# Seven products instead of eight in the down projection of two more chunks, with weights cast in place and later loads

## Chip, cores and metric

One core of one Trainium2 chip (trn2). The metric is the device time of the whole kernel in microseconds (us). A time quoted as a median is the median of a kernel's runs; a span or a duration comes from one profiled execution.

## The reference, cut to what matters

```python
def reference(A_x, A_k_cache, A_v_cache, A_wq, A_wo, B_x, B_w_gate, B_w_up, B_w_down):
    # x: 2048 x 448; 16 query heads, 8 K/V heads of width 256; F = 1792
    xn = layernorm(x)
    # attention: softmax((xn @ wq) k^T / 16) v over the last 512 keys, then @ wo
    s = attention(xn, k_cache, v_cache, wq, wo)
    g = silu((gelu(xn @ w_gate) * (xn @ w_up)) @ w_down)
    return x + s * g
```

The change concerns `... @ w_down` (the "down" product, 1792 to 448), with its silu, called the gates below. The 2048 tokens are worked on in four chunks, 0 to 3, of 512.

## The kernel before

One program lists operations; a helper works out the waits from the buffers that each operation reads and writes. Every engine then carries out its own list in that order. The order in the text is therefore the order in each engine's queue. In the cuts `bank` is the memory into which TensorE writes its results; an eviction is an operation of VectorE or ScalarE that reads a finished bank, after which the bank can be used again.

The plan is: gate and up products of all four chunks, with the down products of chunks 0 and 1 in between; then attention, head by head, for each chunk. The down products of chunks 2 and 3 come in the first two heads of attention, to give TensorE work until the first softmaxes are done.

Chunks 0, 2 and 3 use the plain form, four tiles of 128 tokens with 14 matmuls of 448 columns each:

```python
def down(c, pairs):
    for t4 in range(4):
        ...
        mms([(bank[b][:, 0:D], actT[:, c % 2, f, t4 * P:(t4 + 1) * P], wd[:, f, :], f == 0, f == NF - 1)
             for f in range(NF)], [b_wd] + b_actT[c % 2], (b_ps[b],))
        act(tmp[:, s, 0:D], bank[b][:, 0:D], ACT.Tanh, ...)      # ScalarE
        K.op("dve", ...)                                         # VectorE: the gate
        dma("sp", g2d[t], g2w[t4], ...)
```

Chunk 1 already uses seven products of half size in place of eight (Strassen's scheme in Winograd's form). Some products take sums of activation blocks (`sd`) or of weight blocks (`wdt` 3 to 6), which VectorE makes ahead. `product` is 14 matmuls of 224 columns:

```python
def down7(c, one, other):
    ...
    product(0, B1, A(0, 0))
    act(U2, bank[B1][:, 0:D], ACT.Copy, (b_ps[B1],), bU2, scale=F)   # ScalarE copies product 0
    product(5, B6, S(2))
    product(6, B7, S(3))
    product(3, B4, A(1, 1))
    product(4, B5, S(0))
    product(2, B3, S(1))
    product(1, B1, A(1, 0), False)                                   # adds to product 0's bank
    ... # VectorE evictions, ScalarE tanh, gates
```

A head's scores: four tiles, each of which ScalarE exponentiates into one of three f32 buffers and VectorE then normalizes; the tile is transposed by a DMA on SP's queue. The products with V of a head come two heads later (`LAG = 2`).

```python
def s_mm(m):
    for t4 in range(4):
        b = AB[t4]
        mms([... qT, kT ...], ..., (b_ps[b],))
        n = m * 4 + t4
        r, z, y, x = n % NRS, n % NP32, n // 2 % NPN, n // 4 % NPT       # NP32 = 3
        # ScalarE: p32[:, z, :] = exp(bank[b])
        if t4 % 2 == 1:
            # VectorE: reciprocal of two sums; pn[:, y, t, :] = p32 * reciprocal, for both tiles
            dma_t(pT[...], pn[...], ...)                                # SP: transposed copy
...
for m in range(NS):
    if m in groups:                      # 0, 4, 12, 18, ...: a query stage for the next heads
        ... q_group(...)
    s_mm(m)
    if m < LAG:
        down(NQC - LAG + m, nxt)         # chunks 2 and 3
    ...
    if len(late) == LAG:
        pv(late.pop(0))
```

The softmax here doesn't subtract the row's maximum and nothing guards it: scores larger than these inputs give would overflow.

## Time and profile before

| | before |
|---|---|
| median (3 runs, 545.04 to 546.44) | 546.26 us |
| profiled span | 543.6 us |
| TensorE busy | 538.5 us, 99% |
| down stage of chunk 1 (seven products) | 9.50 us |
| down stages of chunks 2 and 3 (plain) | 10.59 us each |
| heads 2 and 3, up to the second query stage | 7.00 us |

First the busy times by engine and the chain of waits that ended last, from the page of the kernel before:

```profile
PE 538.5 (99%) x4022; PEld 298.2 (55%) x4022; DVE 361.6 (67%) x803; ACT 311.9 (57%) x780; POOL 39.2 (7%) x78
PE 95%; DMA 2%; DVE 1%; ACT 1%; issue 0%; DVEq 0%; ACTq 0%
```

TensorE bounds the kernel nearly everywhere. The windows view of the kernel before, over the stages that the change touches; columns: stretch, its length and PE's busy time in it, then PEld, DVE, ACT, POOL with counts, PE's clock, DMA share, GB/s:

```profile
78.81:88.31 9.50, 9.50 (x101) 9.32 (x100) 6.96 (x12) 3.52 (x7) 0.00 (x0) 1.00 0.01 3
120.37:130.96 10.59, 10.59 (x57) 5.48 (x56) 3.96 (x9) 3.06 (x9) 0.00 (x0) 1.00 0.51 119
132.69:143.28 10.59, 10.59 (x57) 5.48 (x56) 3.96 (x9) 3.12 (x9) 0.00 (x0) 1.00 0.34 92
143.28:150.28 7.00, 7.00 (x33) 3.04 (x32) 4.49 (x12) 6.10 (x19) 2.92 (x5) 1.00 0.46 106
```

Rows are chunk 1's stage, chunk 2's, chunk 3's, and heads 2 and 3. PE is busy throughout, at full clock. The seven-product stage is 1.09 us shorter than a plain one. Two places in the timeline of before: VectorE's last weight sum for chunk 1, and ScalarE around head 1's last two exponentials:

```profile
80.35 0.96 DVE L368 TENSOR_TENSOR wdt<-wdt 128x1568 f16<-128x1568 f16 x1
132.80 0.61 ACT L817 ACTIVATE p<-bank 128x512 f32<-128x512 f32 x1
133.67 0.60 ACT L817 ACTIVATE p<-bank 128x512 f32<-128x512 f32 x1 [0.17 <-DVE pn L824]
135.53 0.54 ACT L365 ACTIVATE tmp<-bank 128x448 f32<-128x448 f32 x1 [1.18 <-PE bank L374]
```

The weight sum ends at 81.31, 2.5 us after the stage began; product 3, which reads it, comes fourth and does not wait. The fourth exponential waits 0.17 us for a normalization (`pn`) that frees its f32 buffer.

### The profile page before, as it was taken

How to read it: one execution, taken by the hardware profiler on the slowest of the kernel's cores; microseconds unless marked ns; L12 is line 12 of the kernel's file. 1: busy time of each engine (PE TensorE's matmuls, PEld its weight loads, DVE VectorE, ACT ScalarE, POOL GpSimd, SP SyncE). 2: the span in 40 equal slices, each digit the busy share in tenths (PEclk: the TensorE clock that was granted, in tenths of full speed). 3: DMA queues.
4: the chain of work that ended last, by engine and by line, in shares of the span. 5: the costliest groups of instructions: out<-in, count | busy, mean ns of one | idle time of the engine just before them, and what ended most of it. 6: DMA issues, size and time to landing. Idle time of an engine off the chain costs nothing.

```text
span 543.6 us, 10604 instructions
## 1 busy us (share of the span) xinstructions
PE 538.5 (99%) x4022; PEld 298.2 (55%) x4022; DVE 361.6 (67%) x803; ACT 311.9 (57%) x780; POOL 39.2 (7%) x78
## 2 busy tenths in 40 slices
PE   8999999999999999999999999999999999999997
PEld 5554457445444444884444469544444984444487
DVE  6673886783457757844775786367667844776775
ACT  5433664873448858206875860488488116877820
POOL 1130400000100000003001000120000003001010
PEclk9999999999999999999999999999999999999999
DMA  9569272993345716402961760068447403773811
GB/s 297 122 189 126 56 128 88 291 237 87 88 93 116 156 44 150 79 1 69 164 156 42 144 151 1 18 145 147 97 105 154 62 1 78 161 150 83 153 49 35
DMA packets 171459, 61.36 MB, mean 113 GB/s; under 512 B 154960, under 2 KB 168272, under 8 KB 171408
## 3 DMA queue, kind: packets, MB, share of 16 engines
q1 hardware_dynamic: 167632, 51.39, 44.4%
q0 software_dynamic: 3008, 8.72, 6.9%
q8 instruction: 32, 0.52, 0.4%
q10 hardware_dynamic: 768, 0.57, 0.3%
q14 instruction: 19, 0.16, 0.1%
HBM read 19.76 MB, written 3.67 MB: 43 GB/s over the span
## 4 chain that ended last, share of the span: by engine, by line
PE 95%; DMA 2%; DVE 1%; ACT 1%; issue 0%; DVEq 0%; ACTq 0%
PE bank L374 95%; DMA pT<-pn 2%; ACT p L817 1%; DVE pn L824 1%; DMA x<-in_A_x_dram 0%; DVE stats L421 0%; ACT qT L365 0%; PE bank L472 0%; DVE rden L821 0%; DVE oTh L842 0%; ACT oTh L365 0%; DVE xn L447 0%; ACT xnT L365 0%; DVE mv L424 0%; PE bank L491 0%
## 5 line engine op out<-in xcount | busy, mean ns | idle before, releaser
L817 ACT ACTIVATE p<-bank 128x512 f32<-128x512 f32 x256 | 150.4, 596 | 25.2 <-DVE pn L824 22.4
L374 PE MATMUL bank<-kT,qT 128*128 128x512 bf16 x512 | 121.1, 379 | 0.0
L374 PE MATMUL bank<-pT,va 128*128 128x512 bf16 x512 | 120.8, 379 | 0.2 <-DMA pT<-pn 0.2
L824 DVE TENSOR_SCALAR pn<-p,rden 128x512 bf16<-128x512 f32 x256 | 113.0, 484 | 9.2 <-DMA pT<-pn 4.9
L374 PE MATMUL bank<-xnT,wq 64*128 64x512 bf16 x768 | 94.9, 376 | 0.0
L374 PE MATMUL bank<-xnT,wgu 64*128 64x512 bf16 (+2 forms) x768 | 84.0, 350 | 0.1
L374 PEld LDWEIGHTS bank<-kT,qT 128*128 128x128 bf16 x512 | 49.3, 98 | 62.0 <-issue 3.8
L374 PEld LDWEIGHTS bank<-pT,va 128*128 128x128 bf16 x512 | 49.7, 98 | 61.2 <-DMA pT<-pn 2.1
L365 ACT ACTIVATE qT<-bank 128x512 bf16<-128x512 f32 x76 | 44.1, 596 | 55.0 <-PE bank L374 53.4
L802 DVE CAST qT<-bank 128x512 bf16<-128x512 f32 x52 | 35.0, 691 | 54.2 <-PE bank L374 54.2
L374 PEld LDWEIGHTS bank<-xnT,wq 64*128 64x128 bf16 x768 | 36.7, 94 | 46.3 <-ACT p L817 1.7
L374 PEld LDWEIGHTS bank<-xnT,wgu 64*128 64x128 bf16 x768 | 37.0, 94 | 36.7 <-issue 0.6
L821 DVE RECIPROCAL rden<-rsum 128x2 f32<-128x2 f32 x128 | 21.2, 166 | 49.8 <-ACT p L817 49.7
L817 ACT ACTIVATION_READ_ACCUMULATOR p<-bank 128x1 f32 x256 | 51.6, 202 | 0.0
L365 ACT ACTIVATE gl<-bank 128x512 bf16<-128x512 f32 x56 | 33.2, 597 | 30.2 <-PE bank L374 26.1
L374 PE MATMUL bank<-wt,sr 128*128 128x224 f16 x512 | 49.7, 259 | 0.0
L374 PEld LDWEIGHTS bank<-wt,sr 128*128 128x128 f16 x512 | 49.1, 98 | 0.0
L365 ACT ACTIVATE xnT<-bank 128x224 bf16<-128x224 f32 (+2 forms) x12 | 4.4, 398 | 71.5 <-PE bank L374 70.9
L842 DVE TENSOR_SCALAR oTh<-bank 128x512 f16<-128x512 f32 x62 | 42.4, 683 | 0.0
L365 ACT ACTIVATE oTh<-bank 128x512 f16<-128x512 f32 x66 | 38.9, 589 | 4.6 <-PE bank L374 4.6
L374 PE MATMUL bank<-wt,oTh 128*128 128x224 f16 x384 | 38.3, 259 | 0.3 <-ACT oTh L365 0.3
L374 PEld LDWEIGHTS bank<-wt,oTh 128*128 128x128 f16 x384 | 36.7, 98 | 1.8 <-ACT oTh L365 1.1
(67 smaller groups left out, 381.9 us busy)
## 6 DMA issues: line engine op xcount, KB each, us to landing
wtb<-in_A_wo_dram POOLq DMA_DIRECT2D x4, 896.0 KB, 10.7
wq<-in_A_wq_dram SPq DMA_DIRECT2D x2, 1536.0 KB, 7.2
va<-in_A_v_cache_dram SPq DMA_DIRECT2D x8, 256.0 KB, 5.6
pT<-pn SPq DMA_TRANSPOSE x128, 2.8
xr<-in_A_x_dram POOLq DMA_DIRECT2D x15, 112.0 KB, 2.3
wd<-in_B_w_down_dram SPq DMA_DIRECT2D x1, 1568.0 KB, 7.5
g<-g_all POOLq DMA_DIRECT2D x14, 112.0 KB, 2.3
out_dram<-xr POOLq DMA_DIRECT2D x12, 112.0 KB, 2.1
```

What stands on the lines that cost most here:

```text
L365: K.op("act", lambda e, o=o, i=i: e.activation(o, i, func, scale=scale), reads, writes)
L374: ins = e.matmul(o, lhsT=l, rhs=r, start=st, stop=sp, skip_group_check=True)
L802: K.op("dve", lambda v, s=s, b=b: v.tensor_copy(qT[:, s, 1, :], bank[b + 1]), (b_ps[b + 1],), (b_qT[s][1],))
L817: K.op("act", lambda e, b=b, r=r, z=z: e.activation(p32[:, z, :], bank[b], ACT.Exp, scale=att_scale, accum_out=rsum[:, r:r + 1]), (b_ps[b] ...
L821: K.op("dve", lambda e, r=r: e.reciprocal(rden[:, r - 1:r + 1], rsum[:, r - 1:r + 1]), b_rsum[r - 1:r + 1], b_rden[r - 1:r + 1])
L824: K.op("dve", lambda e, r=r - 1 + t, z=(n - 1 + t) % NP32, y=y, t=t: e.tensor_scalar(pn[:, y, t, :], p32[:, z, :], rden[:, r:r + 1], None, ...
L842: K.op("dve", lambda v, i=i, b=b: v.tensor_scalar(oTh[:, i, :], bank[b], WS, None, op0=ALU.mult), (b_ps[b],), (b_oT[i],))
```

## The change

Intent: give chunks 2 and 3 the seven-product form too. As no plain down product comes after chunk 0, four of w_down's blocks can be cast to f16 in w_down's own place. The freed and borrowed memory holds the sums. K and V of groups 2 (V: 3) to 7 use memory that chunks 2 and 3 now need, so their loads move into the second query stage. The product order is also changed, in all three stages. The core of the diff (memory layout and helper bodies cut):

```diff
+            product(3, B4, A(1, 1))
+            product(1, B1, A(1, 0), False)
             product(5, B6, S(2))
             product(6, B7, S(3))
-            product(3, B4, A(1, 1))
             product(4, B5, S(0))
             product(2, B3, S(1))
-            product(1, B1, A(1, 0), False)
+            sums(0, B1, None, None)          # f32 part, then tanh on ScalarE
+            gate(0, 0, 0)
             plus(U2, bU2, B6, U2, bU2)
             plus(U3, bU3, B7, U2, bU2)
-  ... (three f32 parts, two tanh tiles, gates delayed by one step)
+            sums(1, B4, U3, bU3)
+            gate(1, 1, 0)
+            sums(2, B5, U3, bU3)
+            plus(U2, bU2, B5, U2, bU2)
+            gate(2, 1, 1)
+            store(1)
+            sums(3, B3, U2, bU2)
+            # then gate(3, 0, 1); store(0)
 ...
-                    for g in range(Hkv):
+                    for g in range(3):
                         load_v(g)
-                    for g in range(2, Hkv):
-                        load_k(g)
 ...
                     q_group(i, ...)
+                    if m == 0:
+                        for k in range(2):
+                            sum_act(2, 2 * p + k)
+                    if m == Q0 and p == 0:
+                        K.reuse(b_kT[2:] + b_va[3:])
+                        for g in range(2, Hkv):
+                            load_k(g)
+                            if g > 2:
+                                load_v(g)
 ...
             if m < LAG:
-                down(NQC - LAG + m, nxt)
+                down7(NQC - LAG + m, (BB[0], BB[1], AB[2], AB[3], BB[2], BB[3]), g2w, b_g2w)()
+                if m == 0:
+                    ...
+                    for k in range(4):
+                        sum_act(3, k)
```

More of the change, by code (lines that the diff above doesn't have):

```diff
@@ L270, in bass_recurrent_scan__sliding_block_cached__geglu_ffn__prompt_kernel @@
         g2w, _, _ = place("g2w", [P, NXR, D], BF16, at=a)
-        g2w = [g2w[:, i, :] for i in range(NXR)] + [g2[:, 0, :]]
-        b_g2w = sbuf_bufs(a, D * 2, NXR) + b_g2[:1]
+        g2w = [g2w[:, 0:2, :], g2[:, :, :]]
+        b_g2w = sbuf_bufs(a, D * 2, 2) + b_g2
         tmp, a, _ = place("tmp", [P, 2, QC], F32)
@@ L309, in bass_recurrent_scan__sliding_block_cached__geglu_ffn__prompt_kernel, with temp, places @@
         NH = NF // 2
-        b_dn = []
-        def temp(name, shape, dt, at, n):
+        def temp(name, shape, dt, at):
             t, a, a2 = place(name, shape, dt, at=at)
-            b = sbuf_bufs(a, (a2 - a) // n, n)
-            b_dn.extend(b)
-            return t, b, a2
-        wdt, b_wdt, a2 = temp("wdt", [P, 7, NH, N2], F16, b_kT[0].lo, 7)
-        sd, b_sd, a2 = temp("sd", [P, 4, NH, HC], F16, a2, 4)
-        cd, b_cd, a2 = temp("cd", [P, 3, D], F32, a2, 3)
-        th, b_th, a2 = temp("th", [P, 2, D], F32, a2, 2)
+            return t, K.buf(a, a2 - a)
+        wdh, _, _ = place("wdh", [P, NF, D], F16, at=b_wd.lo)
+        SD, CD, TD = NH * HC * 2, D * 4, NH * N2 * 2
+        at2 = b_kT[2].lo
+        new = {j: temp("wdt%d" % j, [P, NH, N2], F16, at2 + i * TD) for i, j in enumerate((3, 5, 6))}
+        wdt = {j: (wdh[:, e * NH:(e + 1) * NH, n * N2:(n + 1) * N2], K.buf(b_wd.lo, NF * D * 2))
+               for j, e, n in ((0, 0, 0), (1, 1, 0), (2, 1, 1), (4, 0, 1))}
+        wdt.update({j: (t[:, :, :], b) for j, (t, b) in new.items()})
+        assert at2 + 3 * TD + CD <= b_kT[-1].hi and 2 * SD + CD <= b_va[-1].hi - b_va[3].lo
+        def places(c, sds, cds, ths):
+            S = [temp("sd%d%d" % (c, i), [P, NH, HC], F16, at) for i, at in enumerate(sds)]
+            C = [temp("cd%d%d" % (c, i), [P, D], F32, at) for i, at in enumerate(cds)]
+            T = [temp("th%d%d" % (c, i), [P, D], F32, at) for i, at in enumerate(ths)]
+            return S, C, T
         g2x, a, a2 = place("g2x", [P, 4, D], BF16, at=at)
         b_g2x = sbuf_bufs(a, D * 2, 4)
+        a_wq = b_va[-1].hi
+        dn = {1: places(1, [a_wq + i * SD for i in range(4)], [a_wq + 4 * SD + i * CD for i in range(2)],
+                        [a_wq + 4 * SD + (2 + i) * CD for i in range(2)])}
         NPT, NPN, NP32 = 3, 3, 3
@@ L332, in bass_recurrent_scan__sliding_block_cached__geglu_ffn__prompt_kernel @@
         a_p = b_pn[0].lo
+        a_v, a_th = b_va[3].lo, at2 + 3 * TD
+        dn[2] = places(2, [b_pT[1][0].lo, b_pT[2][0].lo, a_v, a_v + SD], [a_v + 2 * SD, b_pn[2].lo], [a_th])
+        dn[3] = places(3, [b_actT[0][0].lo + i * SD for i in range(4)], [a_v + 2 * SD, b_pT[2][0].lo], [a_th])
         oT, a, at = place("oT", [P, NCO, QC], BF16, at=b_wgu.hi)
@@ L539, in gu_evac @@
             act(gl[:, s, :], bank[b], ACT.Gelu_apprx_tanh, (b_ps[b],), (b_gl[s],))
-            o = actTh if c == 1 else actT
+            o = actTh if c else actT
             K.op("dve", lambda e: e.tensor_tensor(o[:, c % 2, f, :], bank[b + 1], gl[:, s, :], ALU.mult),
@@ L552, in down, with sum_act @@
                 K.op("dve", lambda e, t4=t4, b=b, s=s: e.scalar_tensor_tensor(
-                    out=g2w[t4], in0=tmp[:, s, 0:D], scalar=1.0, in1=bank[b][:, 0:D],
+                    out=g2w[t4 // 2][:, t4 % 2, :], in0=tmp[:, s, 0:D], scalar=1.0, in1=bank[b][:, 0:D],
                     op0=ALU.add, op1=ALU.mult), (b_tmp[s], b_ps[b]), (b_g2w[t4],))
-                dma("sp", g2d[t], g2w[t4], (b_g2w[t4],), (b_g2d[t],))
+                dma("sp", g2d[t], g2w[t4 // 2][:, t4 % 2, :], (b_g2w[t4],), (b_g2d[t],))
         def cast_wd(j, e, n, i):
             fs = (slice(0, 4), slice(4, NH))[i]
+            o, b = wdt[j]
             fe = slice(e * NH + fs.start, e * NH + fs.stop)
-            act(wdt[:, j, fs, :], wd[:, fe, n * N2:(n + 1) * N2], ACT.Copy, (b_wd,), b_wdt[j:j + 1], scale=WS)
+            act(o[:, fs, :], wd[:, fe, n * N2:(n + 1) * N2], ACT.Copy, (b_wd, b), (b,), scale=WS)
         def sum_wd(o, x, y):
-            add("dve", wdt[:, o, :, :], wdt[:, x, :, :], wdt[:, y, :, :], [b_wdt[x], b_wdt[y]], b_wdt[o:o + 1], ALU.subtract)
-        def sum_act(c, k, i):
-            fs = (slice(0, 4), slice(4, NH))[i]
-            o = lambda e, r: (actTh[:, c, e * NH + fs.start:e * NH + fs.stop, r * HC:(r + 1) * HC],
-                              b_actT[c][e * NH + fs.start:e * NH + fs.stop])
-            S = lambda j: (sd[:, j, fs, :], b_sd[j:j + 1])
+            add("dve", wdt[o][0], wdt[x][0], wdt[y][0], [wdt[x][1], wdt[y][1]], [wdt[o][1]], ALU.subtract)
+        def sum_act(c, k, i=None):
+            fs = {0: slice(0, 4), 1: slice(4, NH), None: slice(0, NH)}[i]
+            o = lambda e, r: (actTh[:, c % 2, e * NH + fs.start:e * NH + fs.stop, r * HC:(r + 1) * HC],
+                              b_actT[c % 2][e * NH + fs.start:e * NH + fs.stop])
+            S = lambda j: (dn[c][0][j][0][:, fs, :], [dn[c][0][j][1]])
             j, (x, bx), (y, by), op = ((3, o(0, 0), o(0, 1), ALU.subtract), (2, o(1, 1), S(3), ALU.subtract),
@@ L573, in sum_act, with down7 @@
             add("dve", S(j)[0], x, y, bx + by, S(j)[1], op)
-        def down7(c, one, other):
-            B1, B4, B6, B7, B5, B3 = one[0], one[0] + 1, one[1], one[1] + 1, other[0], other[0] + 1
+        def down7(c, banks, g, b_g):
+            B1, B4, B6, B7, B5, B3 = banks
+            Ss, Cs, Ts = dn[c]
             F = 1.0 / WS
-            A = lambda e, r: (lambda i: actTh[:, c, e * NH + i, r * HC:(r + 1) * HC], b_actT[c][e * NH:(e + 1) * NH])
-            S = lambda i: (lambda k: sd[:, i, k, :], b_sd[i:i + 1])
+            A = lambda e, r: (lambda i: actTh[:, c % 2, e * NH + i, r * HC:(r + 1) * HC], b_actT[c % 2][e * NH:(e + 1) * NH])
+            S = lambda i: (lambda k: Ss[i][0][:, k, :], [Ss[i][1]])
             U2, U3 = tmp[:, 0, 0:D], tmp[:, 1, 0:D]
@@ L585, in product @@
                 lhs, bx = x
-                mms([(bank[b][:, t * N2:(t + 1) * N2], lhs(i)[:, t * P:(t + 1) * P], wdt[:, j, i, :],
-                      first and i == 0 and t == 0, False) for i in range(NH) for t in range(2)], bx + [b_wdt[j]], (b_ps[b],))
+                mms([(bank[b][:, t * N2:(t + 1) * N2], lhs(i)[:, t * P:(t + 1) * P], wdt[j][0][:, i, :],
+                      first and i == 0 and t == 0, False) for i in range(NH) for t in range(2)], bx + [wdt[j][1]], (b_ps[b],))
             def plus(o, bo, b, V, bV):
@@ L591, in plus, with sums @@
                     out=o, in0=bank[b][:, 0:D], scalar=F, in1=V, op0=ALU.mult, op1=ALU.add), [b_ps[b]] + bV, bo)
+            def sums(q, b, V, bV):
+                x, bx = Cs[q % 2]
+                if V is None:
+                    act(x[:, :], bank[b][:, 0:D], ACT.Copy, (b_ps[b],), (bx,), scale=F)
+                else:
+                    plus(x[:, :], [bx], b, V, bV)
+                y, by = Ts[q % len(Ts)]
+                act(y[:, :], x[:, :], ACT.Tanh, (bx,), (by,), scale=0.5)
             def gate(q, r, n):
@@ L594, in gate @@
                 two = lambda x: x.rearrange("p (t d) -> p t d", t=2)
-                act(th[:, q % 2, :], cd[:, q % 3, :], ACT.Tanh, b_cd[q % 3:q % 3 + 1], b_th[q % 2:q % 2 + 1], scale=0.5)
-                def end():
-                    K.op("dve", lambda e: e.scalar_tensor_tensor(
-                        out=g2x[:, 2 * r:2 * r + 2, n * N2:(n + 1) * N2], in0=two(th[:, q % 2, :]), scalar=1.0,
-                        in1=two(cd[:, q % 3, :]), op0=ALU.add, op1=ALU.mult),
-                        (b_th[q % 2], b_cd[q % 3]), b_g2x[2 * r:2 * r + 2])
@@ L602, in gate @@
-                return end
+                (x, bx), (y, by) = Cs[q % 2], Ts[q % len(Ts)]
+                K.op("dve", lambda e: e.scalar_tensor_tensor(
+                    out=g[r][:, :, n * N2:(n + 1) * N2], in0=two(y[:, :]), scalar=1.0, in1=two(x[:, :]),
+                    op0=ALU.add, op1=ALU.mult), (by, bx), b_g[2 * r:2 * r + 2])
             def store(r):
-                for t in range(2 * r, 2 * r + 2):
-                    dma("sp", g2d[c * 4 + t], g2x[:, t, :], (b_g2x[t],), (b_g2d[c * 4 + t],))
+                for t in range(2):
+                    dma("sp", g2d[c * 4 + 2 * r + t], g[r][:, t, :], (b_g[2 * r + t],), (b_g2d[c * 4 + 2 * r + t],))
@@ L617, in down7 @@
             plus(U3, bU3, B7, U2, bU2)
-            plus(cd[:, 0, :], b_cd[:1], B4, U3, bU3)
-            g0 = gate(0, 1, 0)
-            plus(cd[:, 1, :], b_cd[1:2], B5, U3, bU3)
-            g1 = gate(1, 1, 1)
+            sums(1, B4, U3, bU3)
+            gate(1, 1, 0)
+            sums(2, B5, U3, bU3)
             plus(U2, bU2, B5, U2, bU2)
-            g0()
-            plus(cd[:, 2, :], b_cd[2:], B3, U2, bU2)
-            g1()
+            gate(2, 1, 1)
             store(1)
-            g2_ = gate(2, 0, 1)
@@ L628, in down7, with end @@
-            act(cd[:, 0, :], bank[B1][:, 0:D], ACT.Copy, (b_ps[B1],), b_cd[:1], scale=F)
-            g2_()
-            gate(3, 0, 0)()
-            store(0)
-            return (other[1], one[1]), (one[0], other[0])
+            sums(3, B3, U2, bU2)
+            def end():
+                gate(3, 0, 1)
+                store(0)
+            return end
         def ln_first(t):
@@ L770, in bass_recurrent_scan__sliding_block_cached__geglu_ffn__prompt_kernel @@
                 if DOWN_AT[n + 1] == 1:
-                    cur, nxt = down7(1, cur, nxt)
+                    down7(1, (cur[0], cur[0] + 1, cur[1], cur[1] + 1, nxt[0], nxt[0] + 1),
+                          (g2x[:, 0:2, :], g2x[:, 2:4, :]), b_g2x)()
+                    cur, nxt = (nxt[1], cur[1]), (cur[0], nxt[0])
                 else:
@@ L774, in bass_recurrent_scan__sliding_block_cached__geglu_ffn__prompt_kernel @@
                     cur, nxt = nxt, cur
+                    K.reuse([wdt[j][1] for j in (0, 1, 2, 4)])
                 if DOWN_AT[n + 1] == 1:
-                    K.reuse(b_kT + b_va)
                     for b in [y for x in b_wql for y in x]:
-                        b.old.extend(y for x in b_dn for y in x.readers + [x.writer] if y is not None)
+                        b.old.extend(y for x in dn[1] for _, z in x for y in z.readers + [z.writer])
                     load_wq(0)
@@ L965, in bass_recurrent_scan__sliding_block_cached__geglu_ffn__prompt_kernel @@
         K.reuse([b for y in b_qT[QS - Q0:] for b in y])
+        K.reuse([b for x in dn[2] for _, b in x])
         AB.extend(bk(cur, j) for j in range(4))
@@ L985, in bass_recurrent_scan__sliding_block_cached__geglu_ffn__prompt_kernel @@
             if m < LAG:
-                down(NQC - LAG + m, nxt)
+                down7(NQC - LAG + m, (BB[0], BB[1], AB[2], AB[3], BB[2], BB[3]), g2w, b_g2w)()
+                if m == 0:
+                    K.reuse([b for x in b_pT[1:] for b in x] + b_pn[2:])
+                    K.reuse([b for x in dn[3] for _, b in x])
+                    for k in range(4):
+                        sum_act(3, k)
                 if m == LAG - 1:
+                    K.reuse([b for x in b_pT[2:] for b in x])
                     K.reuse(b_oT + [b for y in b_qT[:QS - Q0] for b in y])
```

## The prediction

> **What bounds the kernel.** TensorE: the profile's first part has it busy 538.5 of 543.6 us, and the chain of waits gives it 95% of the span. After 9.7 us it hardly waits, so a saved product pays fully, but so does every new wait.
>
> **Saved.** In the timeline a plain down stage (56 products of 448 columns) lasts 10.59 us (120.37 to 130.96; 132.69 to 143.28), chunk 1's seven-product stage (98 of 224) 9.50 us (78.81 to 88.31). Two chunks converted: 2 x 1.09 = -2.2 us.
>
> **Added, off TensorE.** Per converted chunk, four activation sums on VectorE: 128x1024 f16 took 0.69 us and 128x768 0.55, so about 1.1 us for 128x1792; nine VectorE evictions and gates of 0.62 instead of four; six ScalarE passes instead of four. Casting w_down in place costs nothing. Their place in the queues matters: VectorE and ScalarE work strictly in order ([...]the trace agrees: no eviction overtakes a stalled one).
>
> **The new product order (0, 3, 1, ...) makes three waits:**
> 1. Chunk 1: product 3 could start at 80.17, but its weight sum runs on VectorE from 80.35 to 81.31. Before, it came fourth. +1.2 us.
> 2. Product 1 adds to product 0's bank, so it must wait for ScalarE's copy of that bank. The copy stands behind the four exponentials of the head just scored. The fourth waits for its f32 buffer (one of three), so for the first tile's normalization on VectorE, now behind activation sums. Chunk 2: casts to 117.07, two sums, two casts, two sums to 122.5, normalization to 123.1, exponential to 123.9, copy to 124.4; product 1 could start at 123.1. +1.35 us.
> 3. Chunk 3, counted from chunk 2's last product: VectorE finishes gates at +3.6, sums at +7.9, normalization at +8.6; then the fourth exponential to +9.2, the copy to +9.8. TensorE reaches product 1 at +4.5. +5.4 us idle.
>
> Sum: +7.9 - 2.2 = +5.7 us.
>
> **After that.** Chunk 3's last gate delays head 2's exponentials by about 2.2 us; score banks come free late: +1 us. The 5.4 us gap may drop TensorE's clock ([...]no such gap in this trace): +0.8 us expected. The later K and V loads issue behind head 3's transposes; issue took 1.3 to 1.8 us per K and 0.8 to 1.0 per V: some 13 us in a query stage of 12.2, starting 3.6 into it. Head 4's probability transposes queue 2 us behind them, against some 1.3 us of slack: +1 us (0 to 3).
>
> **Total** 546.3 + 8.6 = about 555 us, 1.6% slower; 8 in 10: 549 to 559. Faster by over 2%: 0.02; within 2%: 0.75; slower by over 2%: 0.23.
>
> **What would show it.** TensorE idle rises by 7 us or more. Chunk 1's stage lasts about 10.7 us with a wait for a weight sum; chunk 2's 10.85 and chunk 3's 14.9, each waiting for ScalarE's copy after product 3. Head 1's fourth exponential waits about 4 us for VectorE. The clock drops just after the gap. Head 4's value products wait for a transpose.
>
> **What would make it wrong.** If the accumulating product need not wait for the copy, or the sums take much less than 1.1 us, waits 2 and 3 shrink: nearer 544 to 548. If the K transposes hold up the probability transposes longer, it passes 557.

## The result

| | before | after |
|---|---|---|
| median, 4 runs each (range) | 545.74 us (545.04 to 546.44) | 555.12 us (554.78 to 556.20) |
| ratio | | 1.0175, 95% interval 1.0154 to 1.0197 |
| profiled span | 543.6 us | 553.0 us |

Ratios are the mean time of one kernel's runs over that of the other's runs of the same rounds, so they are not quite the ratio of the medians. The result is correct. It is slower, but less than 2% slower.

The page of the kernel after:

```profile
PE 539.5 (98%) x4106; PEld 306.8 (55%) x4106; DVE 375.6 (68%) x823; ACT 313.8 (57%) x784; POOL 39.5 (7%) x78
PE 85%; DVE 8%; ACT 4%; issue 1%; DMA 1%; DVEq 0%; ACTq 0%
```

TensorE's idle time rose from 5.1 to 13.5 us (span less busy time), and VectorE and ScalarE entered the chain. The windows of the same four stages after:

```profile
78.90:89.63 10.73, 9.68 (x100) 9.24 (x99) 5.44 (x9) 3.75 (x7) 0.00 (x0) 1.00 0.01 2
121.69:132.25 10.56, 9.57 (x100) 9.31 (x98) 6.88 (x14) 3.57 (x10) 0.00 (x0) 1.00 0.23 51
133.98:150.99 17.01, 11.57 (x99) 10.56 (x98) 10.62 (x18) 5.13 (x13) 0.00 (x0) 0.80 0.22 59
150.99:159.14 8.15, 7.64 (x34) 2.72 (x33) 6.33 (x16) 5.79 (x17) 2.90 (x5) 1.00 0.51 125
```

Chunk 3's row stands out: 17.01 us, 5.4 of them idle, and a mean clock of 0.80. The timeline of PE after shows each wait, in brackets, with what ended it:

```profile
81.48 1.52 PE L387 MATMUL bank<-wdt,actTh 128*128 128x224 f16 x14 [1.05 <-DVE wdt L381]
125.53 1.51 PE L387 MATMUL bank<-wdh,actTh 128*128 128x224 f16 x14 [0.99 <-ACT tmp L378]
142.26 2.79 PE L387 MATMUL bank<-wdh,actTh 128*128 128x224 f16 x14 [5.43 <-ACT tmp L378]
180.83 1.90 PE L387 MATMUL bank<-pT,va 128*128 128x512 bf16 x8 [0.69 <-DMA pT<-pn]
```

These are product 3 of chunk 1 waiting for the weight sum, product 1 of chunks 2 and 3 waiting for ScalarE's copy (`tmp`) of product 0's bank, and head 4's V products waiting for a transpose. What held the copy in chunk 3 is read by following VectorE and ScalarE; first VectorE, from the last gate of chunk 2:

```profile
135.57 0.62 DVE L620 SCALAR_TENSOR_TENSOR g2w<-th,cd 128x448 bf16<-128x448 f32 x1 [0.71 <-ACT th L378]
136.11 1.08 DVE L381 TENSOR_TENSOR sd<-actTh 128x1792 f16<-128x1792 f16 x1
137.23 1.09 DVE L381 TENSOR_TENSOR sd<-actTh,sd 128x1792 f16<-128x1792 f16 x1
138.35 1.09 DVE L381 TENSOR_TENSOR sd<-sd,actTh 128x1792 f16<-128x1792 f16 x1
139.37 1.08 DVE L381 TENSOR_TENSOR sd<-actTh,sd 128x1792 f16<-128x1792 f16 x1
140.37 0.16 DVE L839 RECIPROCAL rden<-rsum 128x2 f32<-128x2 f32 x1
140.56 0.88 DVE L842 TENSOR_SCALAR pn<-p,rden 128x512 bf16<-128x512 f32 x2
```

Then ScalarE in the same stretch, head 1's third and fourth exponential and the copy:

```profile
136.51 0.60 ACT L835 ACTIVATE p<-bank 128x512 f32<-128x512 f32 x1
141.08 0.60 ACT L835 ACTIVATE p<-bank 128x512 f32<-128x512 f32 x1 [3.88 <-DVE pn L842]
141.67 0.54 ACT L378 ACTIVATE tmp<-bank 128x448 f32<-128x448 f32 x1
```

Four activation sums of 1.1 us stand ahead of the normalization; it ends the 3.88 us wait of the exponential; the copy follows, and TensorE 0.05 us behind the copy. Last, the clock in and after that gap (windows of after):

```profile
137.00:142.26 5.26, 0.00 (x1) 0.01 (x1) 4.76 (x9) 1.32 (x5) 0.00 (x0) 0.75 0.13 44
142.26:144.00 1.74, 1.74 (x10) 1.43 (x11) 0.62 (x2) 0.00 (x0) 0.00 (x0) 0.50 0.67 151
144.00:146.00 2.00, 2.00 (x13) 1.62 (x12) 0.00 (x0) 0.88 (x2) 0.00 (x0) 0.50 0.58 131
148.00:151.00 3.00, 3.00 (x34) 3.00 (x33) 1.69 (x3) 0.58 (x1) 0.00 (x0) 1.00 0.02 5
```

The clock fell to half inside the gap, about 2.8 us after TensorE's last product, and the products after the gap run at half clock (2.79 us instead of 1.5 for product 1).

Where the 9.4 us of the span came from, by how far the trace after lags behind the trace before at the same piece of work (start of after less start of before):

| place | lag, us | gained or lost since the row above |
|---|---|---|
| chunk 1's stage starts (78.91, 78.81) | +0.10 | |
| chunk 1's stage ends (89.63, 88.31) | +1.32 | +1.22 weight sum |
| chunk 2's stage ends (132.25, 130.96) | +1.29 | -0.03: about -1.1 saved, +1.1 copy |
| chunk 3's stage ends (150.99, 143.28) | +7.71 | +6.42: -1.2 saved, +5.6 copy, +2.0 clock |
| second query stage starts (159.14, 150.28) | +8.86 | +1.15 late score banks |
| head 4's scores start (171.34, 162.47) | +8.87 | |
| third query stage starts (199.93, 190.21) | +9.72 | +0.85 transposes |
| span ends (553.0, 543.6) | +9.4 | -0.3 |

The split of chunk 3's row uses 9.39 us for a stage without waits (measured in the last experiment below). The five products after the gap took 8.73 us (142.26 to 150.99) instead of five sevenths of 9.39, 6.71: 2.0 us for the clock. The other 5.6 us are the wait. It is listed as 5.43, because the listed time of a product (1.50) runs 0.16 us past the start of the next one (1.34 later); so a wait in brackets understates the delay a little, as also 1.05 against 1.22 in chunk 1.

### The profile page after: what moved, and what is told of

Read it like the earlier page. It is cut to its first block, busy times and chain, and to the rows that moved or that the text cites. A ratio compares the mean times of both kernels' runs of the same rounds, so it can differ in the third digit from the quotient of the medians.

```text
span 553.0 us, 10793 instructions
## 1 busy us (share of the span) xinstructions
PE 539.5 (98%) x4106; PEld 306.8 (55%) x4106; DVE 375.6 (68%) x823; ACT 313.8 (57%) x784; POOL 39.5 (7%) x78
## 4 chain that ended last, share of the span: by engine, by line
PE 85%; DVE 8%; ACT 4%; issue 1%; DMA 1%; DVEq 0%; ACTq 0%
PE bank L387 84%; ACT p L835 2%; DVE actTh L554 1%; DMA pT<-pn 1%; DVE sd L381 1%; DVE pn L842 1%; DVE wt L381 1%; PE bank L504 1%; DVE cd L605 1%; ACT th L378 1%; DVE wdt L381 0%; DVE qT L820 0%; DVE rden L839 0%; DVE g L620 0%; DVE tmp L605 0%
## 5 line engine op out<-in xcount | busy, mean ns | idle before, releaser
L842 DVE TENSOR_SCALAR pn<-p,rden 128x512 bf16<-128x512 f32 x256 | 113.0, 484 | 10.6 <-DMA pT<-pn 6.2
```

The lines of the kernel that those rows point to most:

```text
L842: K.op("dve", lambda e, r=r - 1 + t, z=(n - 1 + t) % NP32, y=y, t=t: e.tensor_scalar(pn[:, y, t, :], p32[:, z, :], rden[:, r:r + 1], None, ...
```

## The experiments

Theory: nothing is wrong with seven products; the change put new work in front of old work in strictly ordered queues, at three places, and the longest resulting gap also dropped the clock. Rivals: the narrow products or the weights cast in place are slow themselves; the extra VectorE work is too much wherever it stands; the moved loads are the cause. Twelve runs were made, one of them the kernel after again as a control, in three batches, each batch on one chip with its own runs of the kernel before. All gave correct results. For every execution the record also lists the mean granted clock of TensorE, where 1.000 is full clock.

| run | median, us | ratio to before (95% interval) |
|---|---|---|
| e1_order1 | 554.75 | 1.0177 (1.0162 to 1.0192) |
| e2_buffer | 550.41 | 1.0101 (1.0081 to 1.0122) |
| e3_filler | 554.65 | 1.0175 (1.0156 to 1.0193) |
| e4_bank | 551.17 | 1.0115 (1.0098 to 1.0131) |
| a_control (the kernel after) | 555.83 | 1.0185 (1.0169 to 1.0201) |
| e5_loads | 555.20 | 1.0176 (1.0162 to 1.0190) |
| e6_chunk1 | 553.65 | 1.0145 (1.0127 to 1.0163) |
| e7_all | 548.21 | 1.0041 (1.0018 to 1.0064) |
| e10_split | 554.53 | 1.0156 (1.0139 to 1.0174) |
| e11_split_filler | 552.66 | 1.0136 (1.0119 to 1.0153) |
| e8_all_split | 542.99 | 0.9951 (0.9938 to 0.9964) |
| e9_all_q4 | 544.94 | 0.9995 (0.9979 to 1.0012) |

### e1_order1: product 3 fourth again in chunk 1

```diff
+            if c == 1:
+                product(5, B6, S(2))
+                product(6, B7, S(3))
             product(3, B4, A(1, 1))
             product(1, B1, A(1, 0), False)
-            product(5, B6, S(2))
-            product(6, B7, S(3))
+            if c > 1:
+                product(5, B6, S(2))
+                product(6, B7, S(3))
```

> Changed kernel, but in chunk 1 alone products 5 and 6 come before product 3, so that product 3 is fourth again. My theory (product 3 waits for the weight sum on VectorE): chunk 1's stage falls from 10.72 to about 9.5 to 9.6 us and the whole by 1.1 to 1.2, to about 554.0 us; chunks 2 and 3 as in the changed kernel, 10.56 and 17.0 us. Rival (seven products at 224 columns from weights cast in place are slower by themselves): the stage stays near 10.7 and the time at 555.1.

The stage fell to 9.50 us (78.86 to 88.36) as expected, which rules out slow narrow products or slow weights cast in place. The time did not follow: 554.75 us, ratio 1.0177 against the 1.0175 of the kernel after. With this order the serial chain of gates ends later, and the second pair of units after the stage had to wait for a bank (timeline of PE in e1_order1):

```profile
93.25 0.82 PE L387 MATMUL bank<-xnT,wgu 64*128 64x512 bf16 x6 [0.83 <-DVE cd L605]
```

So the wait was real, but most of it moved. A miss of the expected total, for a reason that the expectation did not have.

### e2_buffer: a fourth f32 buffer for one exponential

Head 1's fourth exponential gets a buffer of its own, in memory that is idle then.

```diff
-                K.op("act", lambda e, b=b, r=r, z=z: e.activation(
-                    p32[:, z, :], bank[b], ACT.Exp, ...
-                    (b_ps[b],), (b_p32[z], b_rsum[r]))
+                f32 = lambda n: (p32x[:, :], b_p32x) if n == 7 else (p32[:, n % NP32, :], b_p32[n % NP32])
+                K.op("act", lambda e, b=b, r=r, o=f32(n)[0]: e.activation(
+                    o, bank[b], ACT.Exp, ...
+                    (b_ps[b],), (f32(n)[1], b_rsum[r]))
 ... (place of p32x; the normalization reads f32(n) too)
```

> Changed kernel, but head 1's fourth exponential writes a fourth f32 buffer, so it needs no normalization first. Theory (activation sums hold up the normalization, that the fourth exponential, that the copy, that product 1): the fourth exponential starts at once after the third, the copy ends about 3.9 us sooner, the gap before product 1 of chunk 3 falls from 5.43 to about 1.5 us, the clock stays at 1.0, chunk 3's stage falls from 17.0 to about 11.0 us, the whole to about 549.1 us. Rival 1 (TensorE waits for the activation sums themselves): the gap moves to a product of a sum but stays about as long, time near 555. Rival 2 (the ScalarE queue is late because of gates alone): no change.

The exponential starts at once, the gap before product 1 of chunk 3 is 1.44 us, the clock stays at 1.00, the stage is 11.0 us (ScalarE line, then PE lines of e2_buffer):

```profile
137.00 0.61 ACT L839 ACTIVATE p32x<-bank 128x512 f32<-128x512 f32 x1
138.19 1.51 PE L390 MATMUL bank<-wdh,actTh 128*128 128x224 f16 x14 [1.44 <-ACT tmp L381]
149.71 1.76 PE L390 MATMUL bank<-kT,qT 128*128 128x512 bf16 x6 [1.19 <-ACT p L839]
```

One more buffer, of 2 KB in each partition, took away the long wait although every activation sum stayed where it was. Both rivals are out as the cause of the long wait; the 1.44 us that stay are not removed here: the first exponentials of head 1 still stand behind a tanh of chunk 2's gates on ScalarE. Of the expected 6 us 4.0 to 4.7 arrived (ratio 1.0101 against 1.0175; 550.41 against 555.12 us, on another chip): TensorE now met the late exponentials of head 2 sooner, and the wait at head 3's scores grew from 0.23 to 1.19 us.

### e3_filler and e11_split_filler: useless work in the gap

```diff
             product(3, B4, A(1, 1))
+            for i in range(2 if c == 3 else 0):
+                product(3, B5, A(1, 1))      # cleared by product 4 later
             product(1, B1, A(1, 0), False)
```

> Changed kernel, but TensorE runs product 3 of chunk 3 twice more, into a bank that product 4 later clears: 28 more products, 2.7 us of useless work inside the gap. Theory (the gap of 5.43 us halves the clock afterwards, which costs some 2.1 us): the idle gap is about 2.7 us, the clock stays at 1.0, chunk 3's stage falls from 17.0 to about 14.9, the whole to about 553.0 us: faster by added work. Rival (products 1, 5 and 6 of chunk 3 are slow for another reason, such as traffic of VectorE): stage stays 17.0, time 555.1 or more.

In the profiled execution it went as expected: gap 2.75 us, clock 1.00, stage 15.0 us instead of 17.01. But the times scattered (553.5 to 555.88; the profiled one is the 553.5); the three slower executions had a mean clock of 0.996 to 0.997 against its 0.999. It was repeated on top of e10_split (below), which removes another source of scatter:

> The run with split loads, with product 3 of chunk 3 run twice more into a bank cleared later, as in the filler run, now without the scatter of head 4's waits. Theory of the clock: clock 1.0 throughout, chunk 3's stage 15.2 instead of 17.0 to 17.7 us, time 1.8 to 2.5 us below the run with split loads in the same rounds, about 552.3. Rival: no difference in the times, because the useless work delays something else.

Five runs gave 552.13, 552.41, 552.66, 553.97 and 554.03 us; e10_split without the filler 552.93, 554.45, 554.62 and 554.67. The means differ by 1.1 us (554.17 - 553.04). The profiled run is the 554.03, and in it the clock did drop, after a gap of the same length as in e3_filler. The windows of the gap and of what follows, e3_filler first:

```profile
139.67:142.42 2.75, 0.00 (x1) 0.00 (x1) 2.32 (x6) 1.12 (x3) 0.00 (x0) 1.00 0.00 0
142.42:145.00 2.58, 2.58 (x27) 2.58 (x28) 0.63 (x2) 0.99 (x2) 0.00 (x0) 1.00 0.78 178
```

and e11_split_filler:

```profile
139.61:141.50 1.89, 0.00 (x0) 0.00 (x0) 1.85 (x4) 0.33 (x1) 0.00 (x0) 1.00 0.00 0
141.50:142.35 0.85, 0.00 (x0) 0.00 (x1) 0.46 (x3) 0.80 (x3) 0.00 (x0) 0.56 0.00 0
142.35:144.90 2.55, 2.55 (x14) 2.09 (x15) 0.63 (x2) 0.00 (x0) 0.00 (x0) 0.50 0.78 177
145.50:147.60 2.10, 2.10 (x25) 2.10 (x23) 1.16 (x2) 0.80 (x2) 0.00 (x0) 1.00 0.03 8
```

In the same 2.6 us the full clock starts 27 matmuls, the half clock 14. Added work shortens the run where it keeps the clock up; the gain is 1.1 us on average, below the expected 1.8, since it does not do so in every execution. The clocks show this run by run: 1.000 in the three quicker runs (552.13 to 552.66), 0.997 and 0.996 in the two slower ones (553.97 and 554.03), which are 1.6 us longer on average.

### e4_bank: product 1 in a bank of its own

```diff
-            product(1, B1, A(1, 0), False)
+            product(1, B2, A(1, 0), B2 != B1)        # B2 = AB[0] in chunks 2 and 3
-            sums(0, B1, None, None)
+            sums(0, B2, None if B2 == B1 else U2, bU2)
```

> Changed kernel, but in chunks 2 and 3 product 1 goes to the free first score bank instead of adding to product 0's bank; VectorE adds the two. Nothing waits for the ScalarE copy then. Theory: chunk 2's stage 9.5 us (from 10.56); in chunk 3 product 5 waits about 0.3 us for its sum and product 6 about 2 us for its bank, still held by the late fourth exponential; no clock drop; stage 17.0 to about 11.8; whole about 555.1 - 1.1 - 5.2 = 548.8 us. Rival (the accumulation on one bank is not what is waited for): stages stay, time 555.

Chunk 2's stage is 9.4 us; in chunk 3 the two short waits came as forecast, to 0.1 us, the stage is 11.9 us, and the clock held at 1.000 (timeline of PE in e4_bank; the third line is at head 3):

```profile
137.15 1.51 PE L387 MATMUL bank<-wdt,sd 128*128 128x224 f16 x14 [0.21 <-DVE sd L381]
140.60 1.51 PE L387 MATMUL bank<-wdt,sd 128*128 128x224 f16 x14 [1.93 <-ACT p L835]
150.34 1.76 PE L387 MATMUL bank<-kT,qT 128*128 128x512 bf16 x6 [2.09 <-ACT p L835]
```

The accumulation on one bank was what TensorE waited for in both chunks. The total, 551.17 us, misses 548.8 because head 3's scores now wait 2.09 us: head 2's exponentials still stand behind chunk 3's gates. Removing one wait exposes the next.

### a_control and e5_loads: the later loads one step sooner

> The changed kernel itself again, on the chip of the next three, as their measure: 1.0175 times the kernel before, about 554.5 to 555.5 us; stages of chunks 1, 2, 3 at 10.7, 10.56 and 17.0 us; a wait of 0.5 to 1.2 us for a transpose at head 4's value products.

The control repeated the stages (10.7, 10.6, and 17.7 us for chunk 3) but head 4's wait was 2.17 us instead of 0.69, with the loads ending at 177.6 instead of 175.8. This wait differs from execution to execution: 0.44 to 2.17 us in the profiles of the kernels that share this load position. The loads stand in SP's queue ahead of head 4's transposes (timeline of SP in after: the first two and the last of the eleven loads, then the first transpose of head 4):

```profile
163.39 2.64 SPq L375 DMA_TRANSPOSE kT<-in_A_k_cache_dram  x2
175.22 0.58 SPq L372 DMA_DIRECT2D va<-in_A_v_cache_dram  x1
175.91 1.23 SPq L375 DMA_TRANSPOSE pT<-pn  x1
```

```diff
-                    if m == Q0 and p == 0:     # behind head 3's transposes
+            if m == LAG:                       # behind head 2's transposes
                 K.reuse(b_kT[2:] + b_va[3:])
                 ... # the same eleven loads
```

> Changed kernel, but the later K and V loads are issued one step sooner, behind head 2's transposes instead of head 3's. Theory (the loads hold the queue when head 4's transposes are ready): the loads begin about 5 us sooner, head 4's value products wait 0 to 0.3 us instead of 0.7 (0.5 to 1.15 in the profiles so far), time 0.5 to 1.0 us below the control. Rival (head 4's wait comes from the late exponentials of heads 2 and 3): the wait stays at 0.7 and the time at the control's.

A miss. Head 4 did not wait any more, but head 3's V products did, 1.31 us, now that its transposes stood behind the loads:

```profile
177.98 1.90 PE L387 MATMUL bank<-pT,va 128*128 128x512 bf16 x8 [1.31 <-DMA pT<-pn]
```

The time hardly moved (1.0176 against 1.0185, intervals overlap). The rival "late exponentials" is out, since the wait follows the loads; but sooner is not better.

### e10_split: the loads divided over two query stages

```diff
-                    if m == Q0 and p == 0:
+                    if m in (Q0, Q0 + QS) and p == 0:
-                        for g in range(2, Hkv):
+                        for g in range(2, 6) if m == Q0 else range(6, Hkv):
 ... (K.reuse only at m == Q0)
```

> Changed kernel, but of the later K and V only groups 2 to 5 are loaded in the second query stage (seven loads instead of eleven) and groups 6 and 7 in the third. The earlier load position of the last runs only moved the wait to head 3's transposes, so here the queue is left free instead. Theory: loads take 8 us instead of 12.5, end before head 4's transposes are ready, no wait of TensorE for a transpose at heads 3 to 6 (control: 0.4 to 2.2 us), 0.7 to 1.5 us below the control's 555.1 to 555.8, so about 554.4, and less scatter. Rival (head 4's transposes are late because exponentials of heads 2 and 3 are): the wait stays.

No wait of TensorE for a transpose is left in heads 3 to 6, nor in heads up to the first output stage. That follows the loads, so the rival is out. The gain in time is less sure: the ratio is 1.0156, 0.3% or 1.6 us below the control's 1.0185, but the two ran on different chips and their intervals just overlap.

### e6_chunk1: chunk 1's old order, evictions included

Chunk 1 gets back the product order, the three f32 parts and the delayed gates of the kernel before.

> Changed kernel, but chunk 1 has the product order and the order of evictions and gates of the kernel before (three f32 parts instead of two). After the first run of this kind moved the wait from the weight sum to the banks of late gates (0.83 us), both should be gone here: chunk 1's stage 9.5 us, no wait for a bank after it, chunks 2 and 3 at 10.56 and 17.0; time 1.2 us below the control. Rival (w_down cast in its own place costs time in chunk 1): stage above 9.6 us, or less than 0.5 us gained.

The stage is 9.50 us with nothing waiting behind it, and head 0's scores start at 118.83 instead of the control's 119.86. The ratio is 1.0145, 0.4% or 2.2 us below the control: 1.2 us from chunk 1, and in the profiles the rest is head 4's wait, which happened to be 0.44 us. The weights cast in place cost chunk 1 nothing: its stage takes 9.50 us, as it did in the kernel before.

### e7_all, e9_all_q4 and e8_all_split: all three stages mended

Together: chunk 1 as in e6_chunk1. In chunks 2 and 3 product 1 has its own bank and the product into the late score bank comes last; two of chunk 3's sums run on VectorE during chunk 2's products and two after head 1's normalizations; the last two gates come after the next head's exponentials (their parts in f16, to fit in memory). GpSimd's loads of `g` and `x` for the output also start one step later, which the code needs because of the late gates. The three differ only in where the loads of K and V stand.

```diff
+            product(3, B4, A(1, 1))
+            product(1, B2, A(1, 0))
             product(5, B6, S(2))
             product(4, B5, S(0))
             product(2, B3, S(1))
+            product(6, B7, S(3))
+            ... # first two gates, with sum_act(3, 0) and (3, 1) between
+            def tail(): ...                   # last two gates and their store
 ...
             s_mm(m)
+            if m < LAG:
+                for k in range(2, 4):
+                    sum_act(NQC - LAG + m, k)
+            if 0 < m <= LAG:
+                tails.pop()()
```

> All three chunks by seven products without the waits: chunk 1 as before; in chunks 2 and 3 product 1 has a bank of its own and the product of the late bank comes last, two of chunk 3's sums are taken during chunk 2's products and two after the normalizations, the last two gates come after the next head's exponentials, loads one step sooner. Theory: stages of 9.5 us each, heads 2 and 3 in 7.0 us, no clock drop, no wait at head 4; 2 x 1.09 = 2.2 us less than the kernel before, ratio 0.996. Rival (seven products cannot pay here, because the extra work on VectorE must hold up something): ratio 1.000 or above.

The stages were 9.4 to 9.5 us each and heads 2 and 3 waited for nothing, but the loads, as in e5_loads, now made head 3's V products wait 2.94 us, and that gap dropped the clock to 0.50. 548.21 us, ratio 1.0041: a miss caused by the load position alone, as the next two show.

> As the last, but with all eleven loads in the second query stage, where the change put them. They start some 3 us sooner in the stage than in the changed kernel (head 3's transposes are earlier) and take 12.5 us: head 4's value products wait 0 to 1 us; ratio 0.996 to 0.998. If the wait is as long as in the changed kernel (0.4 to 2.2), the load position alone costs what the products save: ratio near 1.000.

With the loads where the change put them the ratio is 0.9995, above the expected 0.996 to 0.998 (five runs at 544.74 to 545.58 us, one at 547.21). The profiled run is the slow one; head 4's V products wait 2.02 us there and then run at half clock (3.56 us instead of 1.9):

```profile
171.71 3.56 PE L393 MATMUL bank<-pT,va 128*128 128x512 bf16 x8 [2.02 <-DMA pT<-pn]
```

> The kernel with all three stages mended (9.4 to 9.5 us each in its trace, heads 2 and 3 in 7.0), whose loads one step sooner made head 3's value products wait 2.9 us with a clock drop; now with the split loads. Theory: no wait for a transpose at heads 3 to 6, clock 1.0; 2.2 us below the kernel before, ratio 0.996, and below both kernels. Rival (the loads cannot be placed later without cost): ratio 1.000 or more.

With the split loads every expected wait is gone. Windows of e8_all_split (chunk 1, chunk 2, chunk 3, heads 2 and 3):

```profile
78.83:88.33 9.50, 9.50 (x101) 9.32 (x100) 6.96 (x12) 3.53 (x7) 0.00 (x0) 1.00 0.01 3
120.39:129.78 9.39, 9.39 (x99) 9.39 (x98) 8.78 (x16) 2.48 (x8) 0.00 (x0) 1.00 0.25 58
131.51:140.90 9.39, 9.39 (x100) 9.39 (x98) 8.65 (x17) 3.61 (x11) 0.00 (x0) 1.00 0.40 106
140.90:147.90 7.00, 7.00 (x34) 3.04 (x33) 6.30 (x15) 6.00 (x18) 0.00 (x0) 1.00 0.40 103
```

542.99 us (542.71 to 543.11), ratio 0.9951: faster than both kernels, at a clock of 1.000 in all six executions, with all the VectorE work of the change still in it (376.3 us busy against 375.6 in the kernel after). The two converted stages save 2 x (10.59 - 9.39) = 2.4 us, and the profiled span is 2.5 us shorter than before (541.1 against 543.6). So neither the seven products nor their extra VectorE work cost anything; what stood between the change and its gain was the order of the queues, together with the shared bank and the place of the loads. The separate worth of each part of this joint mend was not measured.

## Why the prediction was right or wrong

The forecast was 555 us; 555.12 was measured. The exact hit has some luck in it: the kernel before stood at 546.26 us then and at 545.74 with a fourth run, so the forecast difference was 8.6 us and the measured one 9.4. Term by term:

| term of the prediction | forecast, us | measured, us | where |
|---|---|---|---|
| saved by seven products | -2.2 | -2.4 | stages of e8_all_split |
| wait for chunk 1's weight sum | +1.2 | +1.2 | 10.72 - 9.50; removed in e1_order1 and e6_chunk1 |
| wait for the copy, chunk 2 | +1.35 | +1.1 to 1.2 | 10.56 - 9.39 in the stage; removed in e4_bank |
| wait for the copy, chunk 3 | +5.4 | +5.4 to 5.6 | the gap before product 1 (5.43) and the delay; gap 1.44 in e2_buffer |
| clock after the gap | +0.8 | +2.0 (1.5 to 2.7 in six profiles) | five products after the gap, 8.73 - 6.71 |
| late score banks | +1 | +1.15 | 8.15 - 7.00 |
| loads against head 4 | +1 (0 to 3) | +0.85 (0.4 to 2.2 in others) | lag between head 4 and the third query stage |

- Right, and shown by removal: the three waits and their chains. The prediction worked them out from what the trace and the kernel before already hold: durations, the order in each queue, and the buffers' reuse. The activation sums took 1.08 us, forecast about 1.1. The fourth exponential of head 1 waited 3.88 us for VectorE, forecast about 4.
- Right: VectorE and ScalarE work in order. In the trace after, the ready copy of product 0's bank stood 3.88 us behind a waiting exponential.
- Mis-sized: the clock. The prediction treated the drop as uncertain and put only 0.8 us into the sum. That was the author's estimate and rested on no trace: the one of before has no gap of this length. The clock dropped in all six profiles with the 5.4 us gap, and all 24 executions of these six kernels have a mean clock of 0.993 to 0.997. In the kernel after the stage lost 2.0 us by it: it was forecast at 14.9 us and took 17.01. In the total this was hidden by small errors of the other sign (-0.2 us each for the saving, chunk 2's wait and the loads) and by the lower median of the kernel before.
- Right, but only with luck in its size: the loads. Their cost is not a fixed number (waits of 0.44 to 2.17 us); it depends on when eleven loads clear a queue that the transposes share. In e10_split, with four of the loads taken out of the way, TensorE's wait is gone.
- "Casting w_down in place costs nothing" held (9.50 us in e6_chunk1). It could not be tried alone in the kernel before, whose plain products still need the bf16 weights.

## What to carry to other kernels

When work is added to an engine that is not the bottleneck, ask not how much it is but what now stands behind it in that engine's queue, and follow that one chain of buffers to the bottleneck engine: here 4.3 us of sums on an engine that is 67% busy made 4.0 of the 5.4 us of waiting (5.43 - 1.44), because an old reuse of an f32 buffer lay behind them. An accumulation into a bank that another engine must first copy was a wait in chunks 2 and 3, where the second product stood close behind the first (0.99 and 5.43 us in the kernel after, both gone in e4_bank), so put it last or give it its own bank. And after taking away one wait, expect the next one close behind: several of the single repairs here gave less than forecast, and only the joint one gave the whole gain.

## What the runs show of the clock and of the loads

- Gaps shorter than the 5.4 us one were enough to drop the clock. It dropped about 2.0 us after TensorE fell idle in e11_split_filler (gap 2.74 us) and about 2.1 us after it, just as the gap ended, in e9_all_q4 (gap 2.02 us), while similar gaps in e3_filler (2.75 us) and in the control (2.17 us) left it at 1.0. In these kernels a gap of 2 us was already a risk.
- What decides between them was not shown. In nine profiles with a drop the half clock lasted about 3.4 us (e5_loads, e7_all, e9_all_q4, e11_split_filler) or about 6.8 us (the other five).
- In the kernel after the half clock lasted from 139.6 to 146.4 us, and its 4.2 us after the gap cost 2.0, about half of them. In e11_split_filler the full clock came back 2.7 us after TensorE went on (142.35 to 145.02).
- Eleven loads of 256 KB held SP's queue, and with it the transposes issued behind them, for 12.4 us (163.4 to 175.8 in the kernel after), 1.2 to 2.0 us for each transposed K and 0.6 us for each V.
